# A new order table for a one-core DeltaNet and channel-MLP kernel: the same 3,077 steps, other places

## The chip, the cores and the metric

The kernel runs on one core of a Trainium2 chip. The metric is the device time of one execution in microseconds (us), the median of three runs. The core's engines are TensorE (PE, with its weight loads shown as PEld), VectorE (DVE), ScalarE (ACT), GpSimd (POOL) and SyncE (SP), which here issues transfers. Transfers are also issued by ScalarE and GpSimd.

## The reference, cut to what matters

```python
# q, k, v: (B=4, H=8, S=768, D=48); beta: (4, 8, 768); all float32
k_n = k / (np.linalg.norm(k, axis=-1, keepdims=True) + 1e-06)
state = zeros((B, H, D, D))
for t in range(S):
    kt, vt, bt = k_n[:, :, t], v[:, :, t], beta[:, :, t, None]
    y[:, :, t] = einsum('bhd,bhde->bhe', q[:, :, t], state)
    v_old = einsum('bhde,bhd->bhe', state, kt)
    state = state + bt[..., None] * einsum('bhd,bhe->bhde', kt, vt - v_old)
x = y.transpose(0, 2, 1, 3).reshape(B, S, H * D)          # (4, 768, 384)
xn = (x - mean(x)) / sqrt(var(x) + 1e-06) * g_ln
out = x + maximum(xn @ w_ch1, 0.0) @ w_ch2                 # 384 -> 1536 -> 384
```

The first part is a recurrence over 768 tokens with a 48x48 state in each of 32 heads. The second is a layer norm and a two-layer network for each token.

## The kernel before, in words

**Chunks.** The recurrence runs in 12 chunks of 64 tokens (`C = 64`). For each chunk the kernel needs the keys, queries and values, transposed where PE wants them (names kt, qt, kr, tb, v), a Gram matrix of the keys, the inverse of a triangular matrix made from it, and then the chunk's step: `ks` (the state times the keys, L1033), `v - ks` (L1040), `u` (the inverse times that, L1069 and L1074), `y` (the output, L1095, which reads `pt`, the masked product of queries and keys from L851) and `s` (the new state, L1105). After `y` come the layer norm and the network of the chunk (`mlp`), with first-layer products at L1307 or L1407 and second-layer products at L1504.

**The inverse.** `rows_inverse` (from L873) works on two chunks at once, with one pair of head and block in each partition. Loads on SP fill `gb`. Its diagonal is multiplied by beta (L893, with beta from `beta_f` or `beta_b`, and L899); then each of up to 31 columns takes one VectorE product (`tmp`, L909) and one VectorE subtraction (`xb`, L916). Both read two tensors from on-chip memory. The stages are called x0 (first chunk, blocks of 16), x1, x2 and so on. For chunk 0 another way is used at the very start (`first_g` L689 with products at L696, `first_beta` L636, `first_inverse` L708).

**The network in fewer products.** From a certain chunk on the two layers use sums and differences of operands in place of some products. GpSimd makes those sums: L1491 (`h_all`), L1529 (`words`), L1290 (`x_new` and `ident`), and for the weights L1267 (`w_sb`, called W steps). GpSimd also converts loaded weights from words (L603, in `convert`) and issues some transfers (L410, in `dma`), the small `brow` loads (into `u`) and the two `beta_f` loads among them.

**What sets the order.** The kernel body doesn't issue instructions as it goes. `Line.add` (L68) records each piece of work as a numbered step, with its engine, the steps it depends on, and a planned cost. There are 3,077 steps. `Line.emit` (L90) then issues them in the order of a table, the string `ORDER` from L129 on: step numbers, ranges of them (`78-79`), and the letter `f` for a filler matmul (L1582, `zeros`) which computes nothing that is used. `in_this_order` (L25) binds each engine's instructions to that order, and the transfers issued by SP and ACT to one common order among themselves. So the table sets, for each engine, which instruction is behind which.

**Turns on the shared port.** A step can be marked `port`: a VectorE step that reads two tensors from on-chip memory (`port=1`), or one in a mode that uses both ports (`port=2`). In `emit` the first GpSimd step that stands behind such a VectorE step in the table, and is not a transfer, gets a wait for that VectorE step ("shared port"). One VectorE step gives at most one such wait:

```python
                if s.eng == "DVE" and s.plan.get("port"):
                    shared = made[-1]
                if s.eng == "Pool" and "bulk" not in s.plan and shared is not seen:
                    tc.add_manual_dep(
                        made[n], shared.name,
```

So where the table puts several GpSimd steps behind one another with no marked VectorE step between them, only the first of them waits. Nothing in the code makes VectorE wait for GpSimd in the same way.

Of the kernel before, what the change touches and what calls it, by code (L numbers as in the profile page):

```python
# [131 lines left out]
53 391 9 4 6 8 47 250 10 55 54 48 11 52 49 2 62 13 30 56 0 14 26 12 33 7 35 5 58 20 39 18 74 57 251 24 17 59 70 65 1  # L132
37 75 66 91 43 84 41 63 85 80 44 64 32 42 392 81 60 23 76 45 82 46 92 83 19 40 93 34 98 69 29 99 3 15 21 77 86 73 87
94 100 78-79 95 27 96 101 25 102 50 97 88-89 119 103 211 104 16 90 36 113 71 105 38 120 106 114 123 107 72 115 124
108 121 f f f f 125 320 117 28 118 109 126 116 31 128 127 122 307 209 217 110 130 112 111 132 308 227 131 129 310
210 134 22 309 135 f 136 235 204 138 133 142 137 139 141 68 208 140 255 238 205 254 215 144 67 221 143 258 206 146
256 207 145 147 257 148 150 260 322 f 152 149 253 151 158 259 153 398 154 159 155 160 157 321 156 233 163 161 390
242 162 169 218 397 165 164 175 319 222 174 396 168 170 166 171 167 176 173 177-178 172 234 399 244 239 180 236 179
401 185 632 395 51 f 186 261 223 262 182 240 311 400 263 224 181 312 187 393 225 188 61 192 184 243 191 264 183 252
237 212 189-190 394 313 241 314 402 f f 194 193 195-196 226 200 197 265 315 266-267 203 245 213 201 268 357 202 333  # L140
199 633 269-270 198 271 331 316 272-273 219 274 323 275 317 276 220 277 325 362 318 324 228 389 278 326 645 279-280
332 334-335 281 336 282 337 283 327 284 246 285-286 339 338 287-288 355 289 328 290-291 340 329 292 341 343 293 330
403 342 294 346 295 356 296 344 247 231 297 347 298 348 358 f f f 423 767 214 345 353 216 248 464 359 349 422 352
404 354 424 635 465 425 644 350 468 f f f 426 360 303 249 351 304 570 427 305 647 300 367 302 229 361 572 571 301
230 306 574 299 461 573 372 363 637 609 575 232 364-365 428 405 578 388 768 370 467 576 579 368 462 366 463 406 469
369 407 430 466 769 577 773 770 373 634 774 582 408 775 648 371 470-471 777 776 580 472 583 473-474 779 476 475 772
409 581 377 387 586 410 649 477 374 457 584 478 587 375 479 382 480 638 411 636 481 610 585 482-483 376 412 484 639
485-486 646 487 766 590 488 651 413 489 414 490 416 491 588 591 492 378 493-494 611 415 495 380 496 417 379 778 497
589 765 429 381 498 420 383 594 418 650 592 499 419 421 500 640 385 431 501 1062 502 432 503-504 612 780 906 433 595
907 505 434 652 918 436 912 506 435 1074 913 438 1061 507 641 437 771 596 642 1064 597 508 643 441 653 509 439 510  # L150
384 613 654 511 386 614 440 512 655 615 659 616 1076 442 917 513 446 598 1063 443 514 593 660 599 515 459 658 516
1066 600 920 517 601 447 460 518 661 519 656 781 663 520 444 521 657 458 522 617 662 1075 523 618 524 1068 664 525
602 526 1179 527 921 528 448 529 453 624 530 445 531 449 625 922 603 532 456 454 533 452 534 455 535 451 604 536 626
450 665 537-538 782 619 539 620 666-667 605 783 606 668 627 608 813 541 669 621 670-671 540 1065 815 542 1067 543
672-673 1178 674 811 675 816 628 923 676 629 924 821 812 919 914 677 814 678 544 785 819 547 679 1069 607 817 910
820 822 680 546 681-682 784 818 683 1180 548 838 908 684 1550 549 685 911 686 915 827 687 552 835 622 688 551 1181
553 689 623 836 825 550 690 828 916 545 691 554 826 837 833 558 1371 692 557 1078 556 693 555 694 823 695-697 786
925 831 787 698 1184 699 1372 834 700 824 790 701 841 702 1172 839 854 791 703 855 792 1173 1551 788 832 704 1077
1185 705 829 840 559 843 1186 706 856 830 1188 560 707 842 793 1183 708 562 1079 789 561 1073 1177 563-564 709 926
1553 795 1187 710 1080 909 794 711 844 797 845 712 1189 846 713 851 847 1190 714 565 1175 796 715 848 800 798 567  # L160
716 849 569 871 717 1176 801 857 568 718 858 927 566 859 1174 850 872 719 799 720 803 802 721 807 722 928 809 723
806 724 810 725 805 861 808 726 804 727 862 1373 728 863 729 868 864 730 865-866 1552 731 929 852-853 870 732 869
733 1555 930 734 860 931 1191 873 1081 932 879 738 630 736 874 1563 737 880 735 881 1377 933 882 934 883 875-876 884
1070 885 631 877 897 1071 867 878 743 935 1556 1072 1082 1554 1365 937 1565 1379 898 1083 1557 899 886 964 936 900
1084 887 938 888-889 958 890-891 1088 744 892 1366 961 1192 1086 959 740 901 1193 966 1090 939-940 942 968 1087 943
963 967 1093 746 990 941 945 1381 1374 946 1194 969 947 894 1091 747 1375 1378 944 745 902 748 974 741 1567 1558
1092 1195 1182 975 1089 949 739 749 903 1383 1562 1196 972 750 965 753 948 751-752 950 970 991 973 1376 1085 1382
1197 1380 893 742 960 978 1668 1198 954 2054 1201 979 1094 971 1095-1096 951 1199 992 1097 2053 1098 1100 1099 976
1860 1564 1859 1101-1103 980 754 953 977 1104-1105 1200 984 895 1106 904 982 1224 1667 1569 1384 1863 1566 755 1107
993 1368 983 1108 985 981 1385 1109 952 756 1110 996 1111 759 988 2056 1864 1112 1568 1861 1113 986 994 1114 995  # L170
1370 997 999 896 987 1225 1000 989 1001 905 758 1002 757 1009 1673 1006 1010 955 1003 1662 956 998 1011 957 1004
1672 1007 1005 1674 1243 1115 1664 1232 1116 1008 1675-1676 1117 1369 1118-1119 1367 962 1661 1120 1386 1677 1679
1121 1387 1678 1122-1125 760 1126-1127 1570 1016 761 764 1017 763 1128 1026 1129-1130 1018 1131 1012 1132 1019 1133
1013 1024 1027-1029 1228 1030 1014 1020 1015 1239 1031 1134 1021 1023 1034 1135 1035 2058 1036 1032 1037 1136 1226
1038 1041 1039 1042 1025 1043 1229 1033 1137 2066 1227 1138 1022 1040 1139 1203 1052 1389 762 1669 1053 1202 1054
1204 1055 1205-1206 1208 1233 1207 1209 1211-1212 1140 1056 1141 1044 1142 1057 1045 1234 1046 1247 1235 1388 1047
1275 1143 2060 1058 1390 1144 1059 2065 1213 1210 1244 1391 1145 1236 1146 1245 1392 1237 2168 1393 1248 2167 1240
1147 1214 1241 2169 1215 1249 1242 1238 1216 1559 1250 1285 1148 2068 1680 1394 1560 1251 1049 1246 1263 1869 1252
1561 1264 1149 1230 1253-1254 1218 1260 2067 1217 1150 1261 1266 1151 1571 1262 1267 1220 1152 1231 1255 1219 1271
1572 1153 1268 1048 1269 1154 1573 1280 1256 1050 1270 1155 2070 1272 1051 1156-1157 1681 1670 1158 1221 1265 2059  # L180
1222 1159 1276 1671 1277 1273 1160 1274 1682 1286 1281 1257 1161 1278 1577 1287 1578 1162 1279 1694 1288 1581 1223
1258 1576 1289-1290 1582 1294 1303 2166 1291 1417 1304 1428 1060 1292 1282 1295 1313 1296 1293 1283 1314 1297 1315
1259 1300 1305 1871 1306 1316 1310 1163 1317 1580 1318 1298 1418 1301 1319 1419 1338 1299 1339 1302 1307 1340 1311
1308 1167 1330 1166 1309 1312 1331 1284 1332 1575 1333 1432 1165 1320 1574 1321 1579 1322 1334 1327 1164 1335 2171
1323 1424 1336 1324 1696 1858 1325 1328 1345-1346 1665 1337 1326 1341 1583 1342 1584 1666 1585 1347 1586 1348 1663
1421 1343 1857 1349 1344 1350 1873 1587 1683 1396 1422 1588 1395 1356 2170 1351 1436 1357 1589 1329 1868 1684 1358
1872 1425 1590 1426 1170 1352 1420 1359 2069 1685 1360 1423 1361 1687 1437 1591 1688 1397 1438 1686 1362 1427 1433
1399 1865 1429 1400 2367 1866 1592 1430 1404 1870 1689 1451 1431 2055 1874 1434 1405 1593 1875 1594 1439 1460 1398
1435 1595 1168 1445 2072 1401 1596 1446 1364 1597 1465 1441 1598 1447 1452 1448 1599 1693 1470 1449 1363 1440 1692
# [1540 lines left out]
```

## Time and profile before

| | us |
|---|---|
| median of 3 runs | 544.18 |
| lowest and highest | 541.73 and 544.94 |
| the profiled execution's own time | 543.88 |
| its span | 542.2 |
| granted TensorE clock, mean over the span | 0.972 of full |

The profiled execution is a little longer than its span because the span counts from the first instruction on the core to the last. The views used are these. The page's busy rows give each engine's busy time and share of the span. The slices cut the span into 40 equal parts of 13.6 us and give each engine's busy share in tenths, and the clock that TensorE was granted. The busy times by stretch do the same for stretches that one chooses; their columns are named where they are shown. A timeline gives start, length, engine, line, operation, output and inputs, and in brackets the idle time ahead of the instruction and what ended it. "<-DVE pt L851" means that the wait ended when VectorE had finished `pt` at line 851.

### The profile page before, as it was taken

How to read it: one execution, taken by the hardware profiler on the slowest of the kernel's cores; microseconds unless marked ns; L12 is line 12 of the kernel's file. 1: busy time of each engine (PE TensorE's matmuls, PEld its weight loads, DVE VectorE, ACT ScalarE, POOL GpSimd, SP SyncE). 2: the span in 40 equal slices, each digit the busy share in tenths (PEclk: the TensorE clock that was granted, in tenths of full speed). 3: DMA queues.
4: the chain of work that ended last, by engine and by line, in shares of the span. 5: the costliest groups of instructions: out<-in, count | busy, mean ns of one | idle time of the engine just before them, and what ended most of it. 6: DMA issues, size and time to landing. Idle time of an engine off the chain costs nothing.

```text
span 542.2 us, 22784 instructions
## 1 busy us (share of the span) xinstructions
PE 500.3 (92%) x9930; PEld 454.2 (84%) x9930; DVE 367.7 (68%) x814; ACT 208.9 (39%) x461; POOL 283.1 (52%) x457
## 2 busy tenths in 40 slices
PE   5967898989979995999999999999999999999996
PEld 2755776758769885998998999999999999999996
DVE  6676739999994589696598884678986526335141
ACT  4777564423422422133342353351432613514230
POOL 7006485443646863777637508435354473454744
PEclk9799699999999996999999999999999999999999
DMA  8967588497546775055744057463314531203011
GB/s 145 310 111 172 155 181 182 97 119 136 75 78 165 134 113 96 11 150 145 106 82 78 1 118 184 80 124 45 90 31 98 123 44 51 50 2 86 3 30 30
DMA packets 195972, 54.65 MB, mean 101 GB/s; under 512 B 186136, under 2 KB 189344, under 8 KB 195872
## 3 DMA queue, kind: packets, MB, share of 16 engines
q1 hardware_dynamic: 190112, 40.39, 39.7%
q10 hardware_dynamic: 3552, 9.63, 5.5%
q0 software_dynamic: 2208, 3.17, 3.2%
q8 instruction: 78, 1.28, 1.0%
q14 instruction: 22, 0.18, 0.1%
HBM read 36.38 MB, written 16.78 MB: 98 GB/s over the span
## 4 chain that ended last, share of the span: by engine, by line
PE 69%; DVE 15%; DMA 5%; SPq 4%; issue 3%; POOL 2%; DVEq 0%; ACT 0%; POOLq 0%
PE f L1504 23%; PE f L1307 22%; DVE tmp L909 6%; PE f L1407 5%; SPq L410 4%; PE two L820 3%; DVE xb L916 2%; PE by L1033 2%; DVE qt L916 2%; PE two L1033 2%; PE two L1105 2%; PE by L1095 2%; PE two L1088 2%; PE f L1582 2%; DMA beta_b<-in_beta_dram 1%
## 5 line engine op out<-in xcount | busy, mean ns | idle before, releaser
L1491 POOL TENSOR_TENSOR h_all<-h_all 128x256 f32<-128x256 f32 x99 | 72.6, 748 | 35.7 <-PE f L1504 13.8
L1504 PE MATMUL f<-w_sb,h_all 128*128 128x192 f32 x396 | 85.4, 335 | 0.8 <-POOL h_all L1491 0.8
L1504 PE MATMUL f<-words,h_all 128*128 128x192 f32 x396 | 80.3, 333 | 1.3 <-POOL h_all L1491 1.1
L1330 DVE TENSOR_TENSOR h_all<-f,h_all 128x512 f32<-128x512 f32 x72 | 48.9, 685 | 31.9 <-PE f L1307 26.1
L1504 PEld LDWEIGHTS f<-words,h_all 128*128 128x128 f32 x396 | 66.4, 193 | 2.9 <-POOL h_all L1491 1.7
L1504 PEld LDWEIGHTS f<-w_sb,h_all 128*128 128x128 f32 x396 | 66.4, 193 | 2.4 <-POOL h_all L1491 1.0
L1529 POOL TENSOR_TENSOR words<-h_all 128x128 f32<-128x128 f32 x66 | 30.3, 476 | 71.6 <-ACT h_all L1334 48.6
L909 DVE TENSOR_TENSOR tmp<-xb,gb 128x31 f32<-128x31 f32 (+19 forms) x139 | 63.6, 457 | 3.6 <-POOL xb L896 0.4
L916 DVE TENSOR_TENSOR xb<-xb,tmp 128x31 f32<-128x31 f32 (+19 forms) x139 | 54.6, 393 | 3.1
L1407 PE MATMUL f<-xnt,w_sb 128*128 128x256 f32 x216 | 50.9, 386 | 0.0
L1325 ACT COPY h_all<-f 128x512 f32<-128x512 f32 x45 | 26.0, 585 | 62.8 <-PE f L1307 47.5
L410 POOL DMA_DIRECT2D tb<-in_k_dram x64 | 42.1, 661 | 7.9 <-DVE kt L800 5.3
L1407 PEld LDWEIGHTS f<-xnt,w_sb 128*128 128x128 f32 x216 | 39.8, 190 | 5.7
L1334 ACT ACTIVATE h_all<-h_all 128x512 f32<-128x512 f32 x54 | 32.7, 626 | 29.1 <-DVE h_all L1330 28.8
L1307 PE MATMUL f<-x_new,w_sb 128*128 128x128 f32 x288 | 41.2, 277 | 0.0
L1307 PE MATMUL f<-xnt,w_sb 128*128 128x128 f32 x288 | 40.6, 278 | 0.3 <-DVE h_all L1330 0.3
L1307 PEld LDWEIGHTS f<-x_new,w_sb 128*128 128x128 f32 x288 | 37.4, 191 | 0.5 <-POOL x_new L1290 0.2
L1307 PEld LDWEIGHTS f<-xnt,w_sb 128*128 128x128 f32 x288 | 36.5, 192 | 0.8 <-DVE h_all L1330 0.4
L1133 ACT COPY x<-by 128x384 f32<-128x384 f32 x23 | 10.5, 479 | 59.6 <-DVE o L1522 44.9
L603 POOL TENSOR_TENSOR w_sb<-words 128x768 uint32<-128x768 uint32 (+1 forms) x11 | 15.2, 1381 | 34.4 <-DMA beta_b<-in_beta_dram 28.4
L1522 DVE TENSOR_TENSOR o<-f,x 128x192 f32<-128x192 f32 x33 | 11.3, 352 | 31.8 <-PE f L1504 29.2
L1504 PE MATMUL f<-w_sb,words 128*128 128x192 f32 x132 | 27.1, 329 | 0.0
(250 smaller groups left out, 979.8 us busy)
## 6 DMA issues: line engine op xcount, KB each, us to landing
words<-in_moe_w_ch_dram ACTq DMA_DIRECT2D x10, 768.0 KB, 6.7
gd<-gsb SPq DMA_DIRECT2D x11, 512.0 KB, 4.5
v<-in_v_dram SPq DMA_DIRECT2D x24, 192.0 KB, 3.8
out_dram<-o SPq DMA_DIRECT2D x48, 96.0 KB, 2.5
kr<-in_k_dram SPq DMA_DIRECT2D x46, 96.0 KB, 3.4
xld<-xlt SPq DMA_DIRECT2D x9, 384.0 KB, 2.7
xnt<-xld SPq DMA_DIRECT2D x36, 96.0 KB, 3.0
tb<-in_q_dram SPq DMA_DIRECT2D x40, 64.0 KB, 3.2
```

Of the source, the lines that this page charges most:

```text
L410: add(eng, cost, lambda: QUEUE[eng].dma_start(out=out_, in_=in_), r, w, bulk=n * ns / 16e3, np=n, **kw)
L909: lambda j=j, n=n, w=w, t=t: nc.vector.tensor_tensor(out=t, in0=xv[:, 0:n, j : j + 1].to_broadcast([128, n, w]), in1=gv[:, j : j + 1, j + ...
L916: "DVE", dve(n * w), lambda t=t, rest=rest: nc.vector.tensor_tensor(out=rest, in0=rest, in1=t, op=ALU.subtract),
L1033: nc.tensor.matmul(dst[half(e), hp, j], src[drows(hp), (e if n else key_half(c, hp, e)) * GP + j], s_all[drows(hp), e, j], start=(n == 0 o ...
L1307: nc.tensor.matmul(wide(p[:, f : f + 128]), w[:, f : f + 128], r, start=start and i == 0, stop=True, skip_group_check=True)
L1325: add("ACT", act(512), lambda: nc.scalar.copy(o, p), pk, ok)
L1330: add("DVE", dve(512), lambda: nc.vector.tensor_tensor(out=o, in0=x, in1=y, op=op), [*xk_, *yk], ok)
L1334: add("ACT", act(512), lambda: nc.scalar.activation(o, o, ACTF.Relu, scale=scale), [], ok)
L1407: nc.tensor.matmul(p[:, 0:TOK], w1_sb[:, t, f * 128 : (f + 1) * 128], xnt[:, t], start=(t == 0), stop=(t == KC - 1))
L1491: add(eng, cost, lambda: e.tensor_tensor(out=out_, in0=x, in1=y, op=op), r, w, port=2 if eng == "Pool" else 1, pr=-2)
L1504: lambda f=f, t=start and f == order[0]: nc.tensor.matmul(p[:, 0:D2], lhs(f), rhs[:, f], start=t, stop=(f == order[-1]), skip_group_check=True
L1529: lambda f=f + i: e.tensor_tensor(out=s3[f], in0=one(0, 0)[0](f), in1=one(1, 0)[0](f), op=ALU.subtract),
```

## The change

Only the string `ORDER` is changed. The steps, their dependences, `emit` and the rule of the turns stay as they are. The new table has 13 fillers (15 before), and 121 GpSimd steps get a shared-port wait (138 before), since these follow from the table. Ten of the pairs of VectorE and GpSimd step are the same in both. Of the waits behind the step that ran at 225 us before, there are 62 (76 before). On its engine a step moves by 3.9 places on PE on the average, 4.6 on VectorE, 3.2 on ScalarE, 5.4 on GpSimd and 8.3 on SP.

The start of the table, to the first inverse of chunk 0 (65 and 66 are the `brow` loads, 60 and 61 the `beta_f` loads, 391 and 392 `beta_b` loads, 77 the beta transposes, 98 and 99 the products of L696, 125 the first inverse product):

```diff
-53 391 9 4 6 8 47 250 10 55 54 48 11 52 49 2 62 13 30 56 0 14 26 12 33 7 35 5 58 20 39 18 74 57 251 24 17 59 70 65 1
-37 75 66 91 43 84 41 63 85 80 44 64 32 42 392 81 60 23 76 45 82 46 92 83 19 40 93 34 98 69 29 99 3 15 21 77 86 73 87
-94 100 78-79 95 27 96 101 25 102 50 97 88-89 119 103 211 104 16 90 36 113 71 105 38 120 106 114 123 107 72 115 124
-108 121 f f f f 125 320 117 28 118 109 126 116 31 128 127 122 307 209 217 110 130 112 111 132 308 227 131 129 310
...
+53 8 52 65 54 10 9 6 11-12 57 0 35 13 43 58 36 41 4 24 18 29 17 55-56 251 5 20 74 59 70 66 1 23 7 64 60 75 45 63 44
+91 47 81 84 92 48 80 49 85 61 77 76 82 62 392 93 86 73 42 87 15 94 27 79 308 209 101 78 39 83 25 2 100 71 21 95 88
+19 40 3 99 37 96 89 98 97 250 102 119 103 14 90 113 69 104 38 22 16 105 120 211 210 106 114 107 121 242 108 115 118
+f f f f f 125 400 116-117 126 122 127 72 109 217 128 208 130 310 123 129 221 394 132 124 131 111 309 f 142 134 393
```

The stretch of x0 (266 is L893, 268 and up are L909 and L916 in turn, 245, 228 and 220 are conversions of L603, 335 and 336 the two halves of chunk 0's `y`):

```diff
-237 212 189-190 394 313 241 314 402 f f 194 193 195-196 226 200 197 265 315 266-267 203 245 213 201 268 357 202 333
-199 633 269-270 198 271 331 316 272-273 219 274 323 275 317 276 220 277 325 362 318 324 228 389 278 326 645 279-280
-332 334-335 281 336 282 337 283 327 284 246 285-286 339 338 287-288 355 289 328 290-291 340 329 292 341 343 293 330
...
+194 262 252 189 263 212 314 195-196 313 200 197 264 315 265 199 267 202 266 245 357 268-269 201 270-271 203 272 316
+273 f 333 274 633 275 198 323 276 317 277 331 278-279 325 318 324 280 332 395 51 326 281 334 362 282 226 f f 336 246
+283 228 335 338 327 284 220 285 337 286 341 635 355 287 767 339 328 288 214 329 289 216 290 360 330 291 340 342 292
```

The stretch around chunk 5's state product (1107 to 1131 are L909 and L916 in turn, odd numbers L909; 993 to 998 and 1006 to 1008, 1025 sums of L1491 and L1529; 1225 a W step; 1243 and 1232 L1290; 1384 `qt`, 1386 `pt`, 1387 `ks5`):

```diff
-993 1368 983 1108 985 981 1385 1109 952 756 1110 996 1111 759 988 2056 1864 1112 1568 1861 1113 986 994 1114 995
-1370 997 999 896 987 1225 1000 989 1001 905 758 1002 757 1009 1673 1006 1010 955 1003 1662 956 998 1011 957 1004
-1672 1007 1005 1674 1243 1115 1664 1232 1116 1008 1675-1676 1117 1369 1118-1119 1367 962 1661 1120 1386 1677 1679
-1121 1387 1678 1122-1125 760 1126-1127 1570 1016 761 764 1017 763 1128 1026 1129-1130 1018 1131 1012 1132 1019 1133
...
+1111 757 1562 1112 1198 1113 760 1224 1114 1199 1115 761 1116 2055 988 1200 1569 1117 999 992 989 1000 1118 762 1384
+1001 1006 763 1002-1003 997 1004 1119 1673 1201 1005 1120 2056 987 1121 764 998 1122 1385 956 1123 1568 957 1124 955
+1009 2053 1125 1010 1675 1126 1026 1007 1027 1127 1008 1128 1016 1129 1017 1566 1018 1130 1019 2058 1386 1677
+1020-1021 1676 1028 1662 1025 1029 1011 1667 1131 1030 1387 1375 1678 1031 1243 1012 1672 1024 1032 1013 1570 1014
```

The other lines of the table change in the same way. Among the larger moves: on GpSimd, among the steps that ran from 161 to 187 us before, the W steps 964 and 965 and the steps 460, 961, 1085, 878, 870, 958 and 869 stand behind one another, where 870 and 869 (L1491) stood earlier before; the sixth chunk's `ks6` (step 1694) stands 52 places later on PE; the loads of the fifth group of keys stand 49 to 56 places later, and their transposes (step 2073) 51 places later.

## The prediction

> **What bounds the kernel now.** I read the busy rows and slices first, then the busy times by stretch, then the timelines where TensorE (PE) stands still.
>
> ```profile
> PE 500.3 (92%) x9930; PEld 454.2 (84%) x9930; DVE 367.7 (68%) x814; ACT 208.9 (39%) x461; POOL 283.1 (52%) x457
> ...
> PE   5967898989979995999999999999999999999996
> ...
> PEclk9799699999999996999999999999999999999999
> ```
>
> TensorE is the bound: from the 17th slice (13.6 us each) to the last but one it is full. Its clock dips in the 2nd, 5th and 16th slices, and in the 16th PE itself falls to 5.
>
> ```profile
> 50.00:61.00 11.00, 7.03 (x233) 6.48 (x237) 10.04 (x36) 5.57 (x13) 4.29 (x5) 0.72 0.53 193
> ...
> 80.00:160.00 80.00, 73.67 (x1738) 57.36 (x1741) 75.96 (x175) 30.21 (x78) 39.23 (x55) 1.00 0.69 116
> ...
> 200.00:225.00 25.00, 18.53 (x205) 17.58 (x203) 21.31 (x35) 4.29 (x12) 13.88 (x20) 0.80 0.43 71
> 225.00:420.00 195.00, 191.88 (x3769) 182.73 (x3770) 149.23 (x327) 70.98 (x151) 105.13 (x181) 1.00 0.45 93
> ```
>
> The columns are the stretch, its length, then PE, PEld, DVE, ACT and POOL. What is lost lies ahead of 225 us: 3.97 us of PE idle at 50, 6.33 at 80 to 160 (there VectorE is 95% busy), 6.47 at 200. Behind 225 only 3.1 are left to win. The worst place, VectorE first, then GpSimd, then PE:
>
> ```profile
> 201.10 5.34 DVE L909 TENSOR_TENSOR tmp<-xb,gb 128x192 f32<-128x192 f32 x1
> 206.48 0.36 DVE L916 TENSOR_TENSOR xb<-xb,tmp 128x192 f32<-128x192 f32 x1
> ...
> 209.43 1.22 DVE L851 TENSOR_TENSOR pt<-two,pmask 128x1024 f32<-128x1024 f32 x1
> ```
> ```profile
> 201.01 0.87 POOL L1529 TENSOR_TENSOR words<-h_all 128x128 f32<-128x128 f32 x2
> 201.83 0.73 POOL L1491 TENSOR_TENSOR h_all<-h_all 128x256 f32<-128x256 f32 x1
> 202.51 1.26 POOL L1267 TENSOR_TENSOR w_sb<-w_sb 128x512 f32<-128x512 f32 x1
> 203.74 2.08 POOL L1491 TENSOR_TENSOR h_all<-h_all 128x256 f32<-128x256 f32 x3
> 205.79 0.44 POOL L1290 TENSOR_TENSOR ident<-xnt 128x128 f32<-128x128 f32 x1
> 206.53 0.62 POOL L1290 TENSOR_TENSOR x_new<-xnt 128x128 f32<-128x128 f32 x1 [0.30 <-DVE tmp L909]
> ```
> ```profile
> 210.70 0.57 PE L1033 MATMUL two<-s_all,kt 48*64 48x48 f32 x12 [5.69 <-DVE pt L851]
> ```
>
> A VectorE product whose neighbours take 0.34 to 0.36 lasts 5.34 while eight GpSimd operations run back to back, and ends only as GpSimd pauses. Behind it in VectorE's order waits pt, on which PE's state product (ks5) waits. After the 5.69 us of idle the granted clock is half from 208.46 to 218.70. The second place is the first chunk's inverse:
>
> ```profile
> 49.24 0.18 DVE L893 TENSOR_TENSOR db_b<-db_b,beta_f 128x16 f32<-128x16 f32 x1 [2.07 <-DMA beta_f<-in_beta_dram]
> ...
> 50.13 1.48 DVE L909 TENSOR_TENSOR tmp<-xb,gb 128x15 f32<-128x15 f32 x1
> ...
> 53.74 0.75 DVE L909 TENSOR_TENSOR tmp<-xb,gb 128x60 f32<-128x60 f32 x1
> 54.53 0.75 DVE L916 TENSOR_TENSOR xb<-xb,tmp 128x60 f32<-128x60 f32 x1
> ...
> 55.45 0.55 DVE L1074 TENSOR_TENSOR u<-two,bnat 128x384 f32<-128x384 f32 x1
> ```
>
> u (L1074) waits through that chain; PE's first output product waits 3.67 us for u, and the clock is half from 54.86 to 65.10.
>
> **The change part by part.** The steps stay the same; only places change (a mean of 4 on PE and 5 on VectorE and GpSimd, 8 on SP), the two fillers that go counting for nothing, as they run where PE waits anyway. The waits for the shared port fall from 138 to 121, 76 to 62 of them behind 225 us. I sum against the profiled execution, 543.88, which is 0.30 below the median 544.18.
>
> *Start (0 to 25 us).* GpSimd issues the two brow loads second and eighth instead of twelfth and thirteenth (6.08 and 6.64; the second lands at 13.15, 6.5 later). Its other copies and loads there go behind. With the eighth place at some 5 us the load lands at 11.5, and the beta transposes (0.75) end near 12.2 instead of 13.49. But the Gram products (L696, 1.16), which filled PE's wait until 10.33, now stand behind beta, a filler (1.03) and the second raw keys (1.61): they end near 16.0, and their VectorE reader, now at 14.51, starts near 15.3. The first inverse product comes 0.8 later. Bounds: 1 earlier (the load lands at once) and 2 later (the key load of ACT, moved behind two copies, ends last).
>
> *The 50 us place.* GpSimd issues beta_f's second half at its 16th place instead of its 25th, where it left at 42.73 behind an idle queue. The 2.07 wait goes; next late is what L899 waits 0.15 for, so 1.92 is won. Two conversions (L603) leave the pair of 0.75: twice 0.53 more against the 0.22 of their neighbours. The conversion beside the 1.48 stays. u comes 1.92 + 1.06 - 0.8 = 2.2 earlier, and PE's gap shrinks to 1.5. If the clock then holds, the L1095 products take 1.1 instead of 2.17; I take half of that, 0.6. With the start: -2.8. Bounds -4.5 (gap gone, the 1.48 too) and +1 (SP loads that part's beta_b 42 places later, and it lands last).
>
> *60 to 200 us.* SP moves another beta_b load behind the second inverse's loads (20 places); VectorE then waits for it or not. GpSimd's conversions move beside VectorE steps with no shared port. I count 2.5 us of conflict on the 80-to-160 chain against 5.2, but the state updates hang on the loads too: 0. Bounds -4 (PE idle here that waits for data is 4.9) and +5 (two loads as late as beta_f was, 2.07 each, and a conflict of 1).
>
> *The stall at 201.* The run of eight is cut by waits on single inverse steps, the W operation (L1267) goes 12 places back, qt and pt stand 13 and 10 places earlier on VectorE, and ks5 12 places later on PE, behind 18 more L1504 steps (0.325 apart in the rows from 203 to 204.5, so 5.85). Between the previous state and ks5 PE has some 11.5 us of work; VectorE needs 7 to 8 to reach pt, including 1.6 of conflicts. A gap of 1.0 to 1.5 is what I leave for late semaphores. Gain: 5.69 less 1.5, and half of the 8.0 us worked at half clock (210.70 to 218.70), 4.0: 8.2; I take 8.0. Bounds: 0 and 9.7. PE is full from here on, so the gain arrives whole at the end. The trace bears on the clock: the 2.01 us gap at 87.7 is followed by no drop, 3.67 and 5.69 are. That the run is the cause I take from the pause that ends it. The Trainium skill ("SBUF — State Buffer", section "SBUF: two separate sides") has the port pair locked for one whole instruction and then free, so that VectorE would wait through one GpSimd instruction, not through eight. By that, cutting the run would bring nothing of the 8.0, and the sum would be 541.4; the trace's 5.34 is longer than any one of the eight (1.26 at most), so I keep the 8.0.
>
> *225 us to the end.* PE's idle put to GpSimd results is 2.7 us in 225 to 420; fewer waits could take 2 of it. Against it, the wide moves: ks6 comes 52 places later on PE, the loads of the fifth group of keys 49 to 56 later on their queues with their transposes 51 later. None has slack to lose in my reading, since its reader moves with it. 0, bounds -2 and +4.
>
> Sum: -2.8 + 0 - 8.0 + 0 = -10.8, so 533.1 profiled and 533.4 by the median.
>
> **The rivals.**
> *The stall moves.* The new GpSimd order still has a run of 8.6 us with no wait (about 185 us), and the same can be met wherever VectorE's port step falls late into such a run. For it: the table knows only planned times. Against it: VectorE has few two-input steps there. Price as before: 5.7 + 4.0, so 533.4 + 9.7 = 543.1.
>
> *The turns cost PE (the slower side).* Each of the 62 waits behind 225 us holds GpSimd's whole queue, the sums that PE's L1504 products read among it, until a VectorE step has ended. Before, 76 such waits left 2.7 us of PE idle, 0.04 each. It decides from 0.26 each (16.2 us for 1% slower); at 0.3 the price is 18.6: 552. For it: PE's table is as tight as GpSimd's. Against it: the row of 1.9 us in three waits is all that PE loses to L1491 now.
>
> *Early losses.* The stall goes, but the start, 60 to 200 and the tail come out near their upper ends (+2, +5, +4): 544.4.
>
> *The clock holds at the start.* Now half clock runs from 13.90 to 20.73 after the 2.40 gap; the new gap runs from about 8.2 to 11.5. I forecast the same drop. If none comes, some 4 us of products take 2: 531.4. The 2.40 gap with a drop behind it speaks against this, the 2.01 gap at 87.7 without one for it. The Trainium skill ("TensorE: Matmul & The Clock Gate", Part 1: The HAM clock gate) puts the idle window ahead of a drop at about 3.4 us, which would let this gap pass; the trace has a drop behind 2.40, so its chance is small.
>
> *The run is not the cause.* The long product is then its own, wherever it stands, and the stall stays: 533.4 + 8.0 = 541.4. Against it: of 170 L909 products only this one lasts over 1.6 us, and it ends with GpSimd's pause. The Trainium skill's lock of one instruction (named above) would give this case.
>
> **How the numbers follow.** Forecast 0.50, clock holds at the start 0.10, stall moves 0.13, run not the cause 0.04, early losses 0.08, turns cost PE 0.15. One measurement of this kernel tells about 1% (5.4 us) from no change: faster is below 538.7, slower above 549.6. Faster: 0.60; same 0.25; slower 0.15. The forecast's own range is 528 to 538.5 (528: the lower bounds of two terms together). The range that leaves out the turns' case and little else is 527 to 548.
>
> **What would show it.** Right: no inverse step of VectorE over 1.5 us near 200, an idle of under 2 us ahead of ks5, the clock at 1.00 in 200 to 225, u's gap under 2 us, db_b not waiting for beta_f. Wrong: another VectorE step of several us beside an unbroken GpSimd run; PE idle put to L1491 above 10 us behind 225; a clock dip in a new slice; PE busy below 73 in the 80 us after the second inverse's start.

## The result, and the profile after

| | changed kernel | kernel before, same chip |
|---|---|---|
| median | 537.82 us (535.85 to 539.14, 4 runs) | 544.39 us (541.73 to 544.94, 4 runs) |
| ratio | 0.9886, 95% interval 0.984 to 0.9932 | |
| profiled execution and its span | 535.85, 534.1 us | 543.88, 542.2 us |
| mean granted clock | 0.983 | 0.972 |

The change makes the kernel 1.1% faster: 6.6 us by the medians, 8.0 by the two profiled executions. Forecast were 10.8. Measured anew, the ratio was 0.9882 (0.9853 to 0.9911), 533.89 against 541.5 us. The ratios here and below are not the quotients of the medians beside them but differ from these by up to 0.4%, and that of a_w leaves out a slow execution (540.76 us, clock 0.971).

All line numbers of the changed kernel are one higher, because its table is one line longer. First the page's busy row, PE's slices and the clock row of the changed kernel:

```profile
PE 496.2 (93%) x9926; PEld 449.9 (84%) x9926; DVE 355.1 (66%) x814; ACT 208.6 (39%) x461; POOL 285.4 (53%) x457
...
PE   5777797998988998999999999999999999999996
...
PEclk9979999999899999979999999999999999999999
```

PE's 5 in the 16th slice is gone, and so are the clock's dips in the 2nd, 5th and 16th slices. There are new dips in the 3rd, the 11th and the 18th. The stretches of the first table again, with the same columns:

```profile
50.00:61.00 11.00, 7.79 (x249) 6.19 (x247) 10.28 (x40) 7.96 (x16) 5.34 (x8) 1.00 0.77 247
...
80.00:160.00 80.00, 71.04 (x1667) 55.23 (x1665) 72.88 (x174) 29.05 (x75) 40.67 (x59) 0.98 0.69 113
...
200.00:225.00 25.00, 23.44 (x473) 22.30 (x475) 22.53 (x46) 5.26 (x13) 21.36 (x28) 1.00 0.34 46
225.00:420.00 195.00, 191.79 (x3733) 183.21 (x3725) 142.39 (x317) 71.64 (x153) 106.23 (x181) 0.98 0.50 101
```

From 200 to 225 us PE works 23.44 us instead of 18.53, at full clock instead of 0.80. GpSimd works 21.36 instead of 13.88, and VectorE nearly the same. From 80 to 160 PE does less than before. PE's timeline has the state product (L1034, was L1033), and 19 us later a new wait:

```profile
209.33 1.15 PE L1034 MATMUL two<-s_all,kt 48*64 48x48 f32 x64 [1.09 <-DVE pt L852]
```
```profile
228.27 1.22 PE L1308 MATMUL f<-xnt,w_sb 128*128 128x128 f32 x8 [1.83 <-POOL w_sb L1268]
```

The wait ahead of ks5 is 1.09 instead of 5.69. But ks5 itself starts at 209.33, hardly earlier than the 210.70 of before. What is new is how much other work PE has done by then. At 226.43 PE waits 1.83 for a W step (1229), and the clock is half from 229.23 to 236.06 behind it. GpSimd's timeline shows why that step is late:

```profile
224.35 1.39 POOL L1268 TENSOR_TENSOR w_sb<-w_sb 128x512 f32<-128x512 f32 x1
226.53 0.46 POOL L1291 TENSOR_TENSOR xnt<-xnt 128x128 f32<-128x128 f32 x1 [0.80 <-DVE xln L1152]
226.94 2.50 POOL L1268 TENSOR_TENSOR w_sb<-w_sb 128x512 f32<-128x512 f32 x2
```

Step 1229 is the first of the last row. The table puts it behind another W step and behind a sum that waits for the layer norm.

**Where the time came from.** From each trace I worked out PE's remaining work: its busy time times the granted clock, fillers left out, added up from the end. The table says how much earlier (minus) or later (plus) a kernel comes to the same remaining work than the kernel before does at the time on top. The traces' work differs by 1 to 2 us in all, since some records are missing, so the rows are good to about that and are read by their steps. Ahead of 70 us, where PE's steps stand in another order, they also swing with the place: -3.8 at 58 and -8.0 at 64 us in the first pair.

| PE's lead, us, at (us of before) | 60 | 80 | 100 | 140 | 180 | 200 | 220 | 230 | 250 | 400 |
|---|---|---|---|---|---|---|---|---|---|---|
| changed, first profiles of both | -4.8 | -6.1 | -4.9 | -1.9 | -2.1 | -2.6 | -11.8 | -11.5 | -6.8 | -8.1 |
| changed, second profiles of both | -3.7 | -4.7 | -2.0 | -0.8 | -0.2 | -0.6 | -9.0 | -9.7 | -8.7 | -9.5 |

In both pairs the changed kernel leads by about 5 to 6 us at 80 us, and by 200 us 2.6 and 0.6 of it are left. Between 200 and 230 us some 9 are gained. Between 230 and 250 the first pair loses 4.7, which is the W step's wait with its half clock; the second loses 1.0.

### The profile page after: what moved, and what is told of

It is laid out like the page before. It is cut to its first block, busy times and chain, and to the rows that moved or that the text cites. A ratio compares the mean times of both kernels' runs of the same rounds, so it can differ in the third digit from the quotient of the medians.

```text
span 534.1 us, 22770 instructions
## 1 busy us (share of the span) xinstructions
PE 496.2 (93%) x9926; PEld 449.9 (84%) x9926; DVE 355.1 (66%) x814; ACT 208.6 (39%) x461; POOL 285.4 (53%) x457
## 3 DMA queue, kind: packets, MB, share of 16 engines
HBM read 36.38 MB, written 16.78 MB: 100 GB/s over the span
## 4 chain that ended last, share of the span: by engine, by line
PE 56%; DVE 18%; SPq 6%; DMA 5%; issue 4%; POOL 2%; DVEq 0%; ACT 0%; POOLq 0%; ACTq 0%
PE f L1505 23%; PE f L1308 21%; SPq L411 6%; DVE tmp L910 5%; DVE xb L917 4%; PE two L821 2%; DMA xt<-xd 2%; PE f L1408 2%; DVE qt L917 1%; DMA tb<-in_q_dram 1%; PE by L1034 1%; PE two L1089 1%; PE by L1096 1%; PE two L1106 1%; PE two L1034 1%
## 5 line engine op out<-in xcount | busy, mean ns | idle before, releaser
L1505 PE MATMUL f<-w_sb,h_all 128*128 128x192 f32 x396 | 81.4, 329 | 0.0
L1505 PEld LDWEIGHTS f<-words,h_all 128*128 128x128 f32 x396 | 65.2, 190 | 2.7 <-POOL h_all L1492 1.1
L1505 PEld LDWEIGHTS f<-w_sb,h_all 128*128 128x128 f32 x396 | 65.1, 190 | 1.1 <-POOL h_all L1492 0.2
L910 DVE TENSOR_TENSOR tmp<-xb,gb 128x31 f32<-128x31 f32 (+19 forms) x139 | 54.7, 393 | 3.8 <-POOL xb L897 0.7
L1408 PE MATMUL f<-xnt,w_sb 128*128 128x256 f32 x216 | 53.0, 393 | 1.6 <-ACT h_all L1417 1.1
L1408 PEld LDWEIGHTS f<-xnt,w_sb 128*128 128x128 f32 x216 | 40.2, 193 | 8.4 <-ACT h_all L1417 1.9
L1308 PEld LDWEIGHTS f<-xnt,w_sb 128*128 128x128 f32 x288 | 37.2, 195 | 2.7 <-POOL w_sb L1268 2.0
L1417 ACT ACTIVATE h_all<-f 128x256 f32<-128x256 f32 x36 | 13.1, 381 | 32.7 <-PE f L1408 32.5
```

The lines of the kernel that those rows point to most:

```text
L910: lambda j=j, n=n, w=w, t=t: nc.vector.tensor_tensor(out=t, in0=xv[:, 0:n, j : j + 1].to_broadcast([128, n, w]), in1=gv[:, j : j + 1, j + ...
L1308: nc.tensor.matmul(wide(p[:, f : f + 128]), w[:, f : f + 128], r, start=start and i == 0, stop=True, skip_group_check=True)
L1408: nc.tensor.matmul(p[:, 0:TOK], w1_sb[:, t, f * 128 : (f + 1) * 128], xnt[:, t], start=(t == 0), stop=(t == KC - 1))
L1417: lambda hk=hk, p=p: nc.scalar.activation(h_all[:, hk] if c <= LNPE else h_all[:, hk].rearrange("p (g i b) -> p i g b", g=2, b=BK), p[:, 0 ...
L1505: lambda f=f, t=start and f == order[0]: nc.tensor.matmul(p[:, 0:D2], lhs(f), rhs[:, f], start=t, stop=(f == order[-1]), skip_group_check=True
```

## The experiments

All times are medians with the kernel before on the same chip, and the ratio is to it. The "kernel before" and the "changed kernel" are named so; an edit is shown as the numbers of the table that move.

**b_again: the kernel before, unaltered.** 

> The kernel before, written out again with the same table. Theory: the 5.34 us VectorE product beside the eight GpSimd operations belongs to the table, so it comes again at the same step, within 0.5 us, with a PE idle of 5 to 6 us ahead of ks5; time 541 to 545. Rival: the stall was an accident of one profiled execution; then the product lasts under 1.6 us here and the time of this profile is near 535.

One execution: 542.32 us. VectorE and then PE:

```profile
199.59 5.37 DVE L909 TENSOR_TENSOR tmp<-xb,gb 128x192 f32<-128x192 f32 x1
```
```profile
209.21 1.09 PE L1033 MATMUL two<-s_all,kt 48*64 48x48 f32 x29 [5.75 <-DVE pt L851]
```

The same step is held for the same time (5.37 and 5.34), beside the same eight GpSimd operations. The stall belongs to the table; it is no accident.

**b_cut: the run is cut in the kernel before.**

```diff
-995 1370 997 999 ... 1674 1243 1115 1664
+995 1370 1115 997 999 ... 1674 1243 1664
```

> The kernel before with one number of the table moved: VectorE step 1115 stands ahead of GpSimd step 997 instead of behind 1243, so 997 waits for it and the run of eight is cut after its second operation. Theory (the run holds the product): the product lasts under 1.6 us, PE's idle ahead of ks5 falls from 5.69 to under 2.5, the clock stays full there, and the time falls by 7 to 9.7, to 535 to 537.5. Rival (the long product is its own, or PE had other things to wait for): it stays over 4 us, or the idle stays, and the time moves by less than 2.

539.4 us, ratio 0.9962 (0.9929 to 0.9996): some 2 us won instead of 7 to 9.7. VectorE from the step that was held to pt, then PE:

```profile
199.22 1.01 DVE L909 TENSOR_TENSOR tmp<-xb,gb 128x192 f32<-128x192 f32 x1
...
200.66 0.78 DVE L909 TENSOR_TENSOR tmp<-xb,gb 128x207 f32<-128x207 f32 x1
201.47 1.33 DVE L916 TENSOR_TENSOR xb<-xb,tmp 128x207 f32<-128x207 f32 x1
202.83 0.79 DVE L909 TENSOR_TENSOR tmp<-xb,gb 128x220 f32<-128x220 f32 x1
203.55 1.21 DVE L1265 SCALAR_TENSOR_TENSOR qt<-w_more,w_sb 128x512 f32<-128x512 f32 x1
204.68 0.90 DVE L916 TENSOR_TENSOR xb<-xb,tmp 128x220 f32<-128x220 f32 x1
205.50 1.21 DVE L851 TENSOR_TENSOR pt<-two,pmask 128x1024 f32<-128x1024 f32 x1
```
```profile
206.77 1.76 PE L1033 MATMUL two<-s_all,kt 48*64 48x48 f32 x64 [3.93 <-DVE pt L851]
```

The long product is gone: 1.01 instead of 5.37. But GpSimd's operations have only been dealt out: now each of five steps waits for one of them (0.78 to 1.33 where 0.34 to 0.39 would do). From the held step's start to pt's end it takes 7.5 us instead of 9.6 (201.10 to 210.65 before). PE's wait falls from 5.75 to 3.93, and the clock is half for 6.83 us instead of 10.24. So the run was the cause of the one long product, and cutting it took away only a third of PE's wait.

**b_pt: pt goes ahead of the held product in the kernel before.**

```diff
-1114 995 ... 1243 1115 1664 ... 1120 1386 1677
+1114 995 ... 1243 1386 1115 1664 ... 1120 1677
```

> The kernel before with one number moved: VectorE's pt for chunk 5 (1386) stands ahead of the held product (1115) instead of five steps behind it. GpSimd's run of eight stays. Theory (the place of pt behind the product is what turns a held VectorE into an idle PE): the product is still held for about 5 us, but PE's idle ahead of ks5 falls from 5.7 to under 1 and the clock stays full; the time falls by 7 to 9.7 against the kernel before. Rival (the delay of the inverse itself comes back at its next reader): the idle appears again before 225 us and less than 3 is won.

539.72 us, ratio 0.998 (0.995 to 1.0009): no gain that can be told. VectorE, then PE:

```profile
201.37 1.22 DVE L851 TENSOR_TENSOR pt<-two,pmask 128x1024 f32<-128x1024 f32 x1
202.50 4.36 DVE L909 TENSOR_TENSOR tmp<-xb,gb 128x192 f32<-128x192 f32 x1
```
```profile
204.66 1.15 PE L1033 MATMUL two<-s_all,kt 48*64 48x48 f32 x64
...
217.13 1.65 PE L1504 MATMUL f<-words,h_all 128*128 128x192 f32 x4 [5.56 <-DVE o L1522]
```

ks5 starts without a wait, 4.5 us earlier than in b_again. The product is held again (4.36). And PE waits 5.56 us a little later, for VectorE's o (L1522), which stands behind the rest of the inverse; GpSimd waits 8.6 us for its turn there. My theory fell and the rival held: what was taken out of VectorE's way here made its next reader wait.

**h_bn: the kernel before up to step 993 (198.6 us), the new order from there on.** The edit takes the first 1,087 steps in the old order and all others in the new one. (The table numbers its steps from 0 to 3078, so there are 3,079 of them and not 3,077.) 

> The kernel before up to GpSimd's step 993 (198.6 us), and the new table's order for all steps behind it. Theory (the gain is made between 198 and 225 us, where the new table lets GpSimd and PE work on while VectorE's inverse runs): the whole gain of the changed kernel or more, 7 to 10 us, ratio 0.981 to 0.988. Rival (it is spread, a part of it from the start): less than 4 us, above 0.992.

537.61 us, ratio 0.9922 (0.9896 to 0.9948): 3.8 us won. It is less than the theory asked for and just inside the rival's figure. PE's timeline:

```profile
210.34 1.15 PE L1033 MATMUL two<-s_all,kt 48*64 48x48 f32 x64 [1.17 <-DVE pt L851]
```
```profile
229.75 1.27 PE L1307 MATMUL f<-xnt,w_sb 128*128 128x128 f32 x8 [1.83 <-POOL w_sb L1267]
```

By the lead against b_again it gains 9.0 between 200 and 230 (+0.4 to -8.6) and loses 4.3 of it by 240 to the W step's wait and the half clock from 230.66 to 237.49. So the gain of the stage is whole, and the loss behind it comes with the new order too. GpSimd's busy time does not set this run apart: it is 16.78 us from 200 to 225, and 16.52 in b_cut and 16.09 in b_pt, which gain only 2.4 and 2.0 between 200 and 230 by the same measure. PE's order does: 124 second-layer products (L1504) stand ahead of ks5 in h_bn and in the changed kernel's traces, and 102 in the kernel before, b_again, b_cut, b_pt and h_nb.

**h_nb: the new order for the same first steps, the old one from there on.** 

> The other half: the steps that the kernel before has issued by 993 in the new table's order, and the old order behind them. Theory: the stall at 201 is there again and nothing of the new start arrives: ratio 0.996 to 1.004. Rival (spread gain): 3 to 5 us faster, 0.990 to 0.994.

544.39 us, ratio 1.0069 (1.0038 to 1.0099), slower by 3 us. Here another VectorE step (1117) is held 4.87 us beside seven GpSimd operations, and PE waits 7.08 ahead of ks5. The time lies outside both expectations. By the lead this run is 5.0 us behind b_again at 200 us already. So it shows no gain of the new order up to 198 us, but the join fits neither table, and the loss is not the price of the first part alone.

**h70: the new order for the first 378 steps only, to 67.5 us.** 

> The kernel before with only its first 378 steps (to the first scores of chunk 1, 67.5 us) in the new table's order, and all others as before. Theory: the earlier beta_f and the shorter first inverse put chunk 0's y 1.5 to 2.5 us earlier, the clock holds at 54 to 65, and 4 to 6 us of it arrive at the end: 0.989 to 0.993. Rival: VectorE's second inverse, 95 % busy from 80 to 160 us, sets the time there whatever the start is, and less than 1.5 us arrives (above 0.997).

542.63 us, ratio 1.0031 (1.0006 to 1.0057). PE's wait for chunk 0's u ends at 51.87 instead of 54.11 in b_again, as the prediction had it. But the second inverse's first product starts at 83.79 instead of 83.54, and its last step at 119.29 instead of 119.11. By the time the rival held: nothing arrives. Its reason is not shown, because the gain is gone before this inverse begins: the clock is half from 60.05 to 66.88, and VectorE waits 2.46 us for ScalarE's `nrm_b` at 78.28 (1.32 in b_again).

**b_noturn and a_noturn: no waits for the shared port,** in the kernel before and in the changed one.

```diff
-                if s.eng == "Pool" and "bulk" not in s.plan and shared is not seen:
+                if s.eng == "Pool" and not self.steps:
```

> The kernel before without any of its 138 waits for the shared port (they guard no data, only the order of the two engines on the port). Theory (a late VectorE makes the turns hold GpSimd, 12.5 us behind the stall, and so PE): GpSimd's 12.5 us wait goes, more of its sums come in time, and the time falls by 2 to 6 in spite of longer inverse steps. Rival (the turns protect the inverse, which leads from 80 to 160 us): the inverse products there lengthen by 5 to 15 in all and the time rises by 3 to 10.

> The changed kernel without its 121 waits for the shared port. Theory: its table has the two engines in step, so no wait holds GpSimd for long, and without them GpSimd runs ahead into the inverses; the time rises by 2 to 8. Rival (the price of the turns that the prediction named, some 0.05 to 0.3 us for each of the 62 behind 225 us): without them 2 to 5 us are won.

b_noturn: 547.36 us, ratio 1.0125 (1.0073 to 1.0177). a_noturn: 550.51, ratio 1.0161 (1.0136 to 1.0186), where the changed kernel has 0.9882; that is 15 us for 121 waits, about twice what was expected at most. In a_noturn, VectorE and PE:

```profile
230.37 7.57 DVE L917 TENSOR_TENSOR xb<-xb,tmp 128x220 f32<-128x220 f32 x1
```
```profile
242.10 1.99 PE L821 MATMUL two<-kt 48*64 48x64 f32 x64 [6.79 <-DVE s_all L1116]
```

One VectorE step lasts 7.57 us instead of 0.4, beside nine GpSimd operations with no pause (229.99 to 237.33) and a transfer issue; the state sum behind it is late, and PE waits 6.79. So the turns protect VectorE and cost PE nothing like what the prediction's slower rival asked for. In b_noturn the rival had the time right and the place wrong: VectorE is busy 75.29 us from 80 to 160 (74.90 in b_again), and by the lead 5.5 us are lost between 220 and 230, where a product lasts 3.75 us (219.94) beside an unbroken run of GpSimd. The expectation for b_noturn also read GpSimd's wait wrongly: behind the stall GpSimd waits 10.0 us for PE (L1504), which itself waits for VectorE, and not for its turn.

**a_again, a_w, a_best: the changed kernel, and repairs of it.** a_w moves one step; a_best has that and two more.

```diff
-1226 1140 ... 1242 1215 1229 1250
+1226 1229 1140 ... 1242 1215 1250
```

> The changed kernel again, unaltered, as the mark for the others on this chip. Theory: its gain against the kernel before is again near 1.1 % (0.984 to 0.993), with the W wait at 226 and a half clock behind it. Rival: the gain of the first measurement was a favourable draw of waits put to issue, and the ratio comes out above 0.995.

> The changed kernel with one number moved: GpSimd's W step 1229 stands right behind 1226, ahead of 1230 and of 1251, which waits for the layer norm. Theory: the new idle of 1.83 us at 226 and the half clock from 229.2 to 236.1 behind it are one loss of 5.2 that the new place of 1229 makes; both go, and the time falls by 4 to 5.5 against the changed kernel, to 532.5 to 534. Rival: PE had the time to lose, or another W step comes last, and less than 2 is won.

> The changed kernel with three repairs: 1229 (W) behind 1226; VectorE's state sum 1393 ahead of the layer norm's 1213, since a PE product waits 1.6 us for it once the W wait is gone; and PE's first-layer product 825 (with ACT's 820) ahead of the inverse product 549, which waits 2.30 us at 129.6 us with a half clock behind it. Theory: the W wait and its clock 5.2, less 1.0 for what comes last then, and 3 of the 4.0 at 129.6 of which half arrives: 5 to 7 us below the changed kernel. Rival: what is saved at 130 is idle again ahead of chunk 3, and only the 3.5 us of the W repair remain.

a_again: 533.89 us, ratio 0.9882 (0.9853 to 0.9911). a_w: 534.66, ratio 0.9831 (0.9768 to 0.9894). a_best: 534.3, ratio 0.9885 (0.9852 to 0.9918). Neither repair can be told from the changed kernel, which was not measured again beside a_w. In a_w the W wait is gone, and the next product waits for the next late thing; in a_best it is a third one:

```profile
228.63 1.16 PE L821 MATMUL two<-kt 48*64 48x64 f32 x64 [1.59 <-DVE s_all L1116]
```
```profile
PE f L1308 <- POOL x_new L1291: 1.4, 1, 1.4
```

And in a_again the same W wait, 1.82 us, comes without a half clock, as PEclk, the third column from the right, shows for 225 to 240 us, first in the changed kernel's first profile, then in a_again's:

```profile
225.00:240.00 15.00, 13.17 (x291) 12.51 (x282) 11.94 (x26) 4.10 (x7) 8.95 (x13) 0.77 0.43 123
```
```profile
225.00:240.00 15.00, 13.18 (x360) 12.46 (x352) 13.85 (x30) 5.11 (x9) 9.04 (x13) 1.00 0.56 171
```

So of the 5.2 us that a_w was to win, 3.4 are lost only in some executions.

**a_nof: the changed kernel without the two fillers ahead of chunk 0's y.**

```diff
-282 226 f f 336 246
+282 226 336 246
```

> The changed kernel without the two fillers ahead of chunk 0's y (336). They compute nothing that is used. Theory (half clock comes when PE idles for more than about half of one 3.41 us window of a fixed grid): the idle at 51.6 grows from 1.5 to about 2.5 in one window, the clock is half from about 55.1 for at least 3.4 us, and the time rises by 0.5 to 3. Rival (only an idle gap as long as the whole window counts, and a gap of 2.5 passes): the clock stays full at 55 and the time moves by less than 0.5.

535.21 us, ratio 0.9877 (0.9799 to 0.9954). The interval is 8 us wide, so the time tells neither the 0.5 to 3 us of the theory nor the rival's nothing. The clock doesn't tell either: in the profiled execution (541.52) PE stood 3.43 us ahead of L1070 with no cause that the profile shows, and the clock was half from 50.10 to 60.34 whatever the fillers did.

## Why the prediction was right, and where it was not

The direction and the range were right (533.4 forecast, 537.82 measured). The sum was 4 us too good against this measurement.

**The start.** u's wait came as costed: u no longer waits for beta_f, the pair of 0.75 is 0.22 each, and PE's wait for u ends 2.1 us earlier (52.01 in a_again, 54.11 in b_again; 2.2 were forecast). The clock held at 55 us in one profile of the changed kernel and was half from 53.50 to 56.92 in the other. The half clock that I forecast behind PE's early gap did not come: the gap is 0.74 and 1.05 us in the two profiles, and the first drop to half clock comes at 27.84 and 26.20. In b_again it comes at 26.09, so the drop at 13.90 belonged to one execution of the kernel before. By the lead at 60 us the start is worth 4.8 and 3.7 us, where I had 2.8.

**60 to 200 us is a step that failed.** I put it at 0. By the lead, 2.2 and 3.1 us are lost here. In the first pair this cancels what the start brought beyond its forecast (2.6 at 200 us, for 2.8), and that is luck; in the second pair 0.6 is left. The second inverse shows where it goes: its last step starts at 119.30 in a_again and 119.11 in b_again, though its first product came 3.1 us earlier (80.42, 83.54). VectorE's two waits in it, in a_again:

```profile
92.15 1.25 DVE L801 STREAM_TRANSPOSE kt<-tb 128x1024 f32<-128x1024 f32 x1 [1.58 <-DMA tb<-in_k_dram]
98.77 0.95 DVE L1116 TENSOR_TENSOR s_all<-s_all,two 128x768 f32<-128x768 f32 x1 [2.70 <-PE two L1106]
```

In the changed kernel's first profile they are 1.32 and 2.74. In the kernel before no wait of VectorE within this inverse is longer than 0.46, in either profile. So VectorE is not too full to use an earlier start (72.65 us busy from 80 to 160 in a_again, 74.90 in b_again): it stands still for a load of keys and for PE's state product, some 4 us together. The prediction named the loads as a danger and set them off against fewer conflicts. Which of the moved steps bring the two waits was not tried. PE's idle from 80 to 160 is 9.0 us instead of 6.3, and 7.5 instead of 4.8 in the second pair.

**The stall at 201** was forecast at -8.0 and brought about -9: right in size. The forecast's signs came true: idle ahead of ks5 1.09, clock 1.00, no inverse step over 1.5 us near 200. Two signs of being wrong came as well: the clock dips in new slices, and PE is busy below 73 us in the 80 us from the second inverse's start (71.04, and 72.53 in a_again; but the kernel before has 71.97 there in its first profile too, and 75.01 in b_again). But the reason was only half right. I made the cut of GpSimd's run the main thing. b_cut and b_pt show that neither the cut (2 us) nor pt's place (within noise) does it. ks5 starts at about the same time in a_again and b_again, 209.33 and 209.21. What the new order does is to give PE products to work on while VectorE makes its way to pt: 22 more of L1504 ahead of ks5 (124 instead of 102), with the GpSimd sums that they read ready in time. The step of the working that fits this is the one with "18 more L1504 steps". h_bn shows that the new order from 198 us on makes the whole gain of the stage. That PE's products ahead of ks5 make it is read from which traces have them. It was not tried by itself, and neither were b_cut's and b_pt's edits together.

**225 us to the end** was 0 with bounds -2 to +4. Measured: +4.7 and -1.3 in one pair, +1.0 and -0.8 in the other. The new wait at 226 is the rival "the stall moves" in small, at a place that I had not named. In the first pair this term is the one that was mis-sized, 3.4 for 0; in the second it is the time up to 200.

**The turns** were priced as a loss by the slower rival (0.04 to 0.3 us each). a_noturn shows the sign to be the other one: without them the kernel is 2.8% slower (1.0161 by 0.9882).

**A rival's sum.** "Early losses" adds its upper ends to 533.4, in which the start stands with -2.8 already. In place of the terms they make 544.18 - 8.0 + 2 + 5 + 4 = 547.2 and not 544.4.

**The lock of the port and the clock's window.** For the lock of one instruction (the Trainium skill, "SBUF — State Buffer", "SBUF: two separate sides"), the trace agrees mostly. I took an inverse step's end less the least time of its shape as its true start; by that estimate, of 64 steps that came over 0.12 us late in the kernel before, 40 got in when one GpSimd operation had ended, 3 behind two and 1 behind eight (in 20 none had ended meanwhile; if an end may lie up to 0.15 us behind the true start, 57 got in behind one and 3 behind none). That one comes again in b_again, and steps held by six to nine come in b_pt, h_nb, b_noturn and a_noturn. So the rule is the common case and not a bound. Why VectorE gets in between two operations at one time and not at another stayed open. For the window of the clock (the Trainium skill, "TensorE: Matmul & The Clock Gate", Part 1), see the last section.

## What to carry to other kernels

A long operation on one engine tells where the port is lost, but not what it is worth: before counting the stall as a gain, ask what the bound engine could do in the meantime, and which reader of the late engine comes next. Time won early does not reach the end by itself: here some 4 us of new waits of VectorE, for a load and for PE, used up an inverse's start that was 3.1 us earlier. Where GpSimd and VectorE share the port and VectorE has the critical chain, waits that make GpSimd take turns were worth 1.3% to 2.8% here.

## What the runs showed of the hardware

**The clock's windows lie on a grid.** All stretches of half clock inside these traces, the first and the last aside, are 3.41, 6.83 or 10.24 us long, and in one execution their starts lie whole multiples of 3.41 apart (before: 13.90, 54.86 and 208.46, which is 12 and 45 times 3.413). Whether a drop follows goes by PE's idle time within one such window, and a gap needn't be 3.4 us long. In the 14 traces 64 windows at full clock are followed by half clock. Among them are all 37 windows with more than 1.82 us of idle and none with less than 0.98; between these bounds 27 drop and some 70 do not, and what decides there is open. In the changed kernel the 1.83 us of idle at 226.43 lie whole in the window that ends at 229.23, and the clock drops there. In a_again a window's edge at 227.57 (53.50 and 51 windows) cuts the same idle, 1.82 us, into 1.13 and 0.69, and nothing drops. In the same way an edge at 88.99 cuts the 2 us gap at 87.7 in the kernel before, of which the prediction said that no drop followed. The Trainium skill ("TensorE: Matmul & The Clock Gate", Part 1) has the window run freely too, which the traces bear out; its advice that only gaps over about 3.4 us hurt is too mild, since 1.83 us cost 6.83 us of half clock. Where the grid lies differs from one execution to the next, and single executions of the kernel before spread from 537.4 to 546.07 us; that this is the whole reason was not shown, since waits that the profile puts to issue differ as well (0 to 3.4 us).

**A VectorE step can be held through nine GpSimd operations** (7.57 us in a_noturn), where its own time is 0.4.
